# Re-timing the transfers and the layernorm of an attention and gate kernel on one core

## The chip, the core and the metric

The kernel runs on one core of a Trainium2 chip. The metric is the device time of one execution in microseconds (us). Times called a span run from the first to the last instruction of one profiled execution. Engines are named as in the profile: PE (matmul), PEld (its weight loads), DVE (vector), ACT (activation), POOL (GpSimd), SP (the sync engine, whose queue issues most DMAs).

## The reference

One input x of 2048 tokens by 512 is normalised, and the result feeds two branches whose product is added to x:

```python
xn = layernorm(x)                                  # over 512, no scale and no shift
q  = xn @ wq                                       # 512 -> 32 heads of 128
k, v = the last W = 512 rows of k_cache, v_cache   # 8 groups, each for 4 heads
p  = softmax(q k^T * 128 ** -0.5)                  # per head, 512 keys, no mask
s  = concat_heads(p v) @ wo                        # 4096 -> 512
g  = silu(silu(xn @ w1) @ w2)                      # 512 -> 1792 -> 512
out = x + s * g
```

Inputs and output are bfloat16.

## The kernel before

**Tiling.** The 2048 tokens are four blocks of 512 (`BLK`), each of four tiles of 128 (`BLKT`). For every block the normalised x lies transposed in `xnT[b]`, with features on partitions. Work is counted in 128 steps: step s handles block b = s // 32 and head h = s % 32.

**What a step does on PE.** `score(s, j)` multiplies query tile j with the keys into `sc_ps`; ACT takes the exp into `p_all[s]` and the row sums into `den[s]`. `normalise` divides `p_all` by the sums on DVE, two tiles at a time. `flip(s)` transposes `p_all[s]` into `pT[s]` by one DMA on the SP queue, issued in step s + 1. `pv_units(s)` multiplies pT with the values; it runs in step s + 3 (`LAG`). `q_units(s + 2)` computes the queries of the step after next. The `p_all`, `qT` and `pT` slots rotate over three buffers.

**Fill.** Between these, `pump(n)` takes matmuls from a list. In the 32 steps of the first block these are the gate branch (`mlp_units`) of blocks 1 to 3: 56 `h_unit` (xn @ w1, 14 chunks of four matmuls, each evacuated by a tanh on ACT and a multiply on DVE into `hT`) and 56 `o_unit` (into `g_sb`) for each block, 10 or 11 per step. In the later steps they are the output matmuls (`out_units`) of the block before, four per step: for each tile 32 heads of oT times wo, then DVE multiplies by the gate and adds x, and the result is stored. The x for that addition (`x_e`) is loaded again by POOL.

**Block 0 ahead of the steps.** Its layernorm runs on loaded tiles, PE transposes them (`turn`, `keep`), and its gate branch runs whole. Warm-up matmuls fill PE until the data are there. The first four chunks of `h` are computed in halves of 256 tokens, so that the first half can start before tiles 2 and 3 are transposed.

**Layernorm.** `stats` is a pair of statistics instructions on DVE; `rstd_of` takes Sqrt on ACT and a reciprocal on DVE; `center` is one DVE instruction per tile; `flip_x` transposes a tile into `xnT` by DMA on SP. Statistics of blocks 2 and 3 run during block 0's gate output; all four centerings and flips of block 2 stand at the end of step 0, those of block 3 at the end of step 1. The x blocks take their buffers from the `pT` slots.

**Loads and order.** `load_head_group(g)` loads keys (a transposing DMA), wq and values of a group on SP; groups 0 to 2 before the steps, the others at the end of the odd steps 1 to 9. `load_wo` loads wo in six parts on POOL's queue into the places that w1, w2 and hT leave. The order on PE, ACT, DVE and SP is written out by hand (`manual_schedule`), each engine executing in that order; POOL's was left to the planner.

Of the kernel before, what the change touches and what calls it, by code (L numbers as in the profile page):

```python
# [9 lines left out]
P = 128  # L10
# [6 lines left out]
LAG = 3  # L17
# [5 lines left out]
def kernel(  # L23
# [41 lines left out]
    make_identity(nc, ident)  # L65
    eps = const.tile([P, 1], FP32, name="eps")
    nc.vector.memset(eps, 1e-5)

    wq_sb = [res.tile([P, ND, REP * DH], BF16, name=f"wq{g}") for g in range(HKV)]
    kT = [res.tile([P, W], BF16, name=f"kT{g}") for g in range(HKV)]  # L70
    v_sb = [res.tile([P, NKC, DH], BF16, name=f"v{g}") for g in range(HKV)]
    xnT = [res.tile([P, ND, BLK], BF16, name=f"xnT{b}") for b in range(NBLK)]
    g_sb = [res.tile([P, BLKT, D], BF16, name=f"g{b}") for b in range(NBLK)]

# [9 lines left out]

    x_blk = {}

    def load_x(b):
        x_blk[b] = work.tile([P, BLKT, D], BF16, name="x_blk", tag="pT", bufs=3)  # L90
        if b == 0:
            for j in range(BLKT):
                nc.sync.dma_start(x_blk[b][:, j, :], x2[ds(j * P, P), :])
        else:
            nc.sync.dma_start(
                x_blk[b], x2[ds(b * BLK, BLK), :].rearrange("(j p) d -> p j d", p=P)
            )

    mv = res.tile([P, NBLK * BLKT, nc.vector.BN_AGGR_DIM], FP32, name="mv")
    rstd = res.tile([P, NBLK * BLKT], FP32, name="rstd")  # L100
# [1 line left out]
    def stats(b, j):  # L102
        st = work.tile([P, nc.vector.BN_STATS_DIM], FP32, name="st", bufs=4)
        nc.vector.bn_stats(out=st, in_=x_blk[b][:, j, :])  # L104
        nc.vector.bn_aggr(out=mv[:, b * BLKT + j, :], in_=st)  # L105

    def rstd_of(t0, n):
        nc.scalar.activation(
            rstd[:, t0 : t0 + n], mv[:, t0 : t0 + n, 1], ACT.Sqrt, bias=eps, scale=1.0
        )  # L110
        nc.vector.reciprocal(rstd[:, t0 : t0 + n], rstd[:, t0 : t0 + n])

    def center(b, j):
        t = b * BLKT + j
# [39 lines left out]
    def mlp_units(b, tag_of):  # L154

        cur = {}

        def h_unit(f, c):
            if (f, c) == (0, 0):
                new_hT(b)  # L160
            if c == 0:
                cur["ps"] = ps.tile([P, BLK], FP32, name="h_ps", tag=tag_of(f), bufs=PS_BUFS[tag_of(f)])
            h_mm(cur["ps"], b, f, c, 0, BLK)
            if c == ND - 1:
                h_evac(cur["ps"], b, f)

        def o_unit(j, f):
            if f == 0:
                cur["ps"] = ps.tile([P, D], FP32, name="oB_ps", tag=tag_of(j), bufs=PS_BUFS[tag_of(j)])
            nc.tensor.matmul(  # L170
                cur["ps"],
                hT[b][f // 2][:, f % 2, j * P : (j + 1) * P],
                w2_sb[f // FH][:, f % FH, :],
                start=(f == 0),
                stop=(f == NFC - 1),
            )
            if f == NFC - 1:

                th = work.tile([P, D], BF16, name="th", bufs=2)
                nc.scalar.activation(th, cur["ps"], ACT.Tanh, scale=0.25)  # L180
                nc.vector.scalar_tensor_tensor(
                    out=g_sb[b][:, j, :], in0=th, scalar=1.0, in1=cur["ps"], op0=ALU.add, op1=ALU.mult
                )

        hs = [lambda f=f, c=c: h_unit(f, c) for f in range(NFC) for c in range(ND)]
        os_ = [lambda j=j, f=f: o_unit(j, f) for j in range(BLKT) for f in range(NFC)]
        return hs, os_

# [80 lines left out]
                return t[:, h - lo, :]  # L269
        raise KeyError(h)  # L270

    def load_wo(lo, n, tag):
        t = reg.tile([P, n, D], BF16, name=f"wo{lo}", tag=tag)
        nc.gpsimd.dma_start(t, A_wo[ds(lo * DH, n * DH), :].rearrange("(h p) n -> p h n", p=P))
        wo_t.append((lo, n, t))

    def out_units(b):
        units = []
# [35 lines left out]
    wqv = A_wq.rearrange("(c p) n -> p c n", p=P)  # L314
    warm = const.tile([P, BLK], BF16, name="warm")
    nc.gpsimd.memset(warm, 0.0)

    with tc.manual_schedule(engines={ENG.PE, ENG.Activation, ENG.DVE, ENG.SP}):

        load_x(0)  # L320
        for i in range(2):
            nc.sync.dma_start(w1_sb[i], w1v[:, :, i * FH * P : (i + 1) * FH * P])
        load_x(1)
        for i in range(2):
            nc.sync.dma_start(w2_sb[i], w2v[:, i * FH : (i + 1) * FH, :])
        load_x(2)
        load_head_group(0)
        load_x(3)
        load_head_group(1)


        warm_ps = ps.tile([P, BLK], FP32, name="warm_ps", tag="o", bufs=1)
# [14 lines left out]

        stats(0, 0)
        stats(0, 1)
        rstd_of(0, 2)  # L350
        center(0, 0)
        center(0, 1)
        stats(0, 2)
        stats(0, 3)
        warm_up(11)
        t0 = turn(0)
        warm_up(2)
        t1 = turn(1)
        keep(nc.scalar, t0, 0)
        keep(nc.vector, t1, 1)  # L360
        warm_up(3)
        rstd_of(2, 2)
        center(0, 2)
        center(0, 3)


        new_hT(0)
        HB = BLK // 2
        NEARLY = 4
        early = [ps.tile([P, BLK], FP32, name="h_ps", tag="sc", bufs=PS_BUFS["sc"]) for _ in range(NEARLY)]  # L370
        for f in range(NEARLY):
            for c in range(ND):
                h_mm(early[f], 0, f, c, 0, HB)
            if f == 2:
                t2 = turn(2)
                t3 = turn(3)
                keep(nc.scalar, t2, 2)
                keep(nc.vector, t3, 3)
# [6 lines left out]
        for i, u in enumerate(hs[NEARLY * ND :]):  # L385
            u()
            f, c = divmod(i + NEARLY * ND, ND)
            if c == ND - 1 and f in (5, 7, 9, 11):
                stats(1, (f - 5) // 2)
        for i, u in enumerate(os_):  # L390
            u()
            if i == 2:
                rstd_of(BLKT, BLKT)
                for j in range(BLKT):
                    center(1, j)
                    flip_x(1, j)
            if i % 6 == 4 and i // 6 < 2 * BLKT:
                b, j = divmod(i // 6, BLKT)
                stats(2 + b, j)
            if i == 40:  # L400
                for q in q_units(0):
                    q()
            if i == 49:
                for q in q_units(1):
                    q()
        rstd_of(2 * BLKT, 2 * BLKT)
        load_head_group(2)


        fill = []  # L410
# [10 lines left out]
                    fill.pop(0)()  # L421
                    done += 1

        wo_plan = {HQ: [(14, 7, "big2")], HQ + 2: [(21, 7, "big3")], HQ + 3: [(28, 2, "pair0"), (30, 2, "pair1")]}
        wo_first = False
        for s in range(NSTEP):
            b, h = divmod(s, HQ)
# [27 lines left out]
            pump(cut[4])  # L455
            score(s, 3)
            pump(cut[5])
            if s in (0, 1):
                for j in range(BLKT):
                    center(2 + s, j)  # L460
                    flip_x(2 + s, j)
            if s % 2 == 1 and 3 + s // 2 < HKV:
                load_head_group(3 + s // 2)
            if not wo_first and b == 0 and done >= n_mlp - BLKT * NFC:
                load_wo(0, 7, "big0")
                load_wo(7, 7, "big1")
                wo_first = True
            for args in wo_plan.get(s, []):
                load_wo(*args)

# [1 line left out]
        s = NSTEP  # L472
        normalise(s - 1, 2, 3)
        flip(s - 1)
        for i in range(LAG):
            for u in pv_units(s - LAG + i):
                u()
            pump(8)
        pump(len(fill))


# [28 lines left out]
```

## Time and profile before

| what | value |
|---|---|
| median of 9 runs | 575.68 us (573.91 to 576.65) |
| profiled execution, its time | 574.93 us |
| its span | 573.2 us |
| PE busy | 549.7 us (96%) |
| DVE busy | 440.8 us (77%) |
| ACT busy | 386.3 us (67%) |
| POOL busy | 21.8 us (4%) |
| queue of SP and other hardware-generated DMAs | 81.29 MB, 74.8% of 16 engines |
| queue of POOL's DMAs | 7.87 MB, 5.2% |

Busy shares are means over the span. The busy tenths show the span in 40 slices of 14.3 us, where 9 means 90% or more. A row of the timeline has the start in us, the duration, the engine, the line, the operation, the tiles, a count, and in brackets the idle time before it and what ended that. SPq and POOL rows of DMAs are the issue, not the transfer; the transfer's end is given as time to landing. The granted clock (PEclk) is 1.00 at full speed.

### The profile page before, as it was taken

The page shows a single profiled execution, that of the slowest core. Times are in us where ns is not written, and L with a number is a line of the kernel's source. Part 1 is how long each engine was busy: PE and PEld are TensorE (multiplying, and loading weights), DVE is VectorE, ACT ScalarE, POOL GpSimd, SP SyncE. Part 2 cuts the span into 40 slices and gives each one's busy share as a digit, 9 for nine tenths or more (in the row PEclk, how much of TensorE's full clock was granted, in tenths as well). Part 3 has the DMA queues.
Part 4 walks back from the last instruction along what each step waited for, and adds up shares of the span by engine and source line. Part 5 has one row for each costly group of instructions (what it writes and reads, how often), then busy time and mean ns, then how long its engine had stood idle before and what let it go on. Part 6 is the DMA issues. An engine that isn't in the chain of part 4 may idle for free.

```text
span 573.2 us, 8179 instructions
## 1 busy us (share of the span) xinstructions
PE 549.7 (96%) x2527; PEld 252.2 (44%) x2576; DVE 440.8 (77%) x1185; ACT 386.3 (67%) x1108; POOL 21.8 (4%) x41
## 2 busy tenths in 40 slices
PE   8987699999999989999999999999999999999897
PEld 4433244444444434444444444444444444444345
DVE  5978467886787658888888878888888888888622
ACT  4657465775686657777777777777777777777400
POOL 0000000000000110000000000000000000000000
PEclk9999799999999989999999999999999999999999
DMA  8926999656578798989888888998988897989900
GB/s 285 248 73 111 192 179 215 119 100 119 108 164 165 134 258 160 166 151 168 157 171 160 169 148 171 156 173 155 173 148 165 151 178 148 180 148 171 166 27 29
DMA packets 293836, 89.68 MB, mean 156 GB/s; under 512 B 282272, under 2 KB 291872, under 8 KB 293792
## 3 DMA queue, kind: packets, MB, share of 16 engines
q1 hardware_dynamic: 291328, 81.29, 74.8%
q0 software_dynamic: 2464, 7.87, 5.2%
q8 instruction: 20, 0.33, 0.2%
q14 instruction: 24, 0.20, 0.1%
HBM read 17.30 MB, written 2.10 MB: 34 GB/s over the span
## 4 chain that ended last, share of the span: by engine, by line
PE 86%; DMA 5%; DVE 5%; ACT 2%; issue 1%; SPq 0%; ACTq 0%
PE sc_ps L222 19%; PE s_ps L286 18%; PE o_ps L254 18%; PE q_ps L203 18%; PE oB_ps L170 6%; PE h_ps L138 6%; DMA pT<-p_all 4%; DVE hT L150 2%; DVE st L104 1%; DMA w<-in_B_w_dram 1%; DVE x_blk L115 1%; ACT th L149 1%; ACT p_all L225 0%; DVE mv L105 0%; DVE p_all L237 0%
## 5 line engine op out<-in xcount | busy, mean ns | idle before, releaser
L225 ACT ACTIVATE p_all<-sc_ps 128x512 bf16<-128x512 f32 x512 | 305.0, 597 | 118.3 <-PE sc_ps L222 106.5
L222 PE MATMUL sc_ps<-kT,qT 128*128 128x512 bf16 x512 | 195.2, 382 | 0.7
L237 DVE TENSOR_SCALAR p_all<-p_all,rden 128x512 bf16<-128x512 bf16 x512 | 158.6, 352 | 9.1
L254 PE MATMUL o_ps<-pT,v 128*128 128x512 bf16 x498 | 135.3, 382 | 9.7 <-DMA pT<-p_all 9.3
L286 PE MATMUL s_ps<-wo,oT 128*128 128x512 bf16 (+1 forms) x533 | 141.3, 368 | 0.6
L203 PE MATMUL q_ps<-xnT,wq 128*128 128x512 bf16 x500 | 134.9, 379 | 0.6 <-DVE qT L212 0.2
L259 DVE CAST oT<-o_ps 128x512 bf16<-128x512 f32 x128 | 88.3, 690 | 50.6 <-PE o_ps L254 48.1
L225 ACT ACTIVATION_READ_ACCUMULATOR p_all<-sc_ps 128x1 f32 x512 | 100.7, 197 | 0.0
L212 DVE CAST qT<-q_ps 128x512 bf16<-128x512 f32 x128 | 87.9, 686 | 3.2 <-PE q_ps L203 3.2
L254 PEld LDWEIGHTS <-v 128*128 128x128 bf16 x512 | 49.9, 98 | 71.3 <-DMA pT<-p_all 6.7
L286 PEld LDWEIGHTS <-oT 128*128 128x128 bf16 x544 | 53.4, 98 | 58.2 <-issue 1.1
L222 PEld LDWEIGHTS <-qT 128*128 128x128 bf16 x512 | 50.4, 98 | 64.6 <-issue 5.3
L203 PEld LDWEIGHTS <-wq 128*128 128x128 bf16 x512 | 50.2, 98 | 61.9 <-issue 2.3
L138 PE MATMUL h_ps<-xnT,w 128*128 128x512 bf16 (+1 forms) x236 | 65.5, 370 | 6.5 <-DVE hT L150 5.5
L170 PE MATMUL oB_ps<-w,hT 128*128 128x512 bf16 x216 | 62.8, 379 | 0.3
L235 DVE RECIPROCAL rden<-den 128x2 f32<-128x2 f32 x256 | 40.6, 159 | 15.8 <-ACT p_all L225 15.8
L150 DVE SCALAR_TENSOR_TENSOR hT<-th,h_ps 128x512 bf16<-128x512 bf16 x56 | 37.6, 682 | 18.8 <-ACT th L149 18.2
L149 ACT ACTIVATE th<-h_ps 128x512 bf16<-128x512 f32 x56 | 33.4, 598 | 9.4 <-PE h_ps L138 7.1
L138 PEld LDWEIGHTS <-w 128*128 128x128 bf16 x240 | 23.6, 99 | 29.8 <-issue 4.8
L170 PEld LDWEIGHTS <-hT 128*128 128x128 bf16 x224 | 21.9, 98 | 26.5 <-DVE hT L150 0.3
L299 DVE TENSOR_TENSOR sg<-s_ps,g 128x512 f32<-128x512 f32 (+1 forms) x17 | 11.1, 655 | 18.4 <-PE s_ps L286 18.4
L180 ACT ACTIVATE th<-oB_ps 128x512 bf16<-128x512 f32 x16 | 9.5, 595 | 15.6 <-PE oB_ps L170 14.7
(28 smaller groups left out, 85.7 us busy)
## 6 DMA issues: line engine op xcount, KB each, us to landing
wq<-in_A_wq_dram SPq DMA_DIRECT2D x8, 512.0 KB, 4.4
w<-in_B_w_dram SPq DMA_DIRECT2D x4, 896.0 KB, 8.8
wo<-in_A_wo_dram POOLq DMA_DIRECT2D x4, 896.0 KB, 8.3
pT<-p_all SPq DMA_TRANSPOSE x128, 4.5
x_e<-in_A_x_dram POOLq DMA_DIRECT2D x16, 128.0 KB, 3.5
x_blk<-in_A_x_dram SPq DMA_DIRECT2D x3, 512.0 KB, 8.2
out_dram<-x_e POOLq DMA_DIRECT2D x12, 128.0 KB, 2.2
v<-in_A_v_cache_dram SPq DMA_DIRECT2D x8, 128.0 KB, 4.4
```

Source lines behind the costliest of these rows:

```text
L138: nc.tensor.matmul(h_ps[:, lo : lo + n], w1_sb[f // FH][:, c, (f % FH) * P : (f % FH + 1) * P], xnT[b][:, c, lo : lo + n], start=(c == 0), ...
L150: nc.vector.scalar_tensor_tensor(out=hT[b][f // 2][:, f % 2, :], in0=th, scalar=1.0, in1=h_ps, op0=ALU.add, op1=ALU.mult)
L170: nc.tensor.matmul(cur["ps"], hT[b][f // 2][:, f % 2, j * P : (j + 1) * P], w2_sb[f // FH][:, f % FH, :], start=(f == 0), stop=(f == NFC - 1),
L203: nc.tensor.matmul(cur["ps"], wq_sb[h // REP][:, c, (h % REP) * DH : (h % REP + 1) * DH], xnT[b][:, c, :], start=(c == 0), stop=(c == ND - 1),
L212: nc.vector.tensor_copy(qT[s], cur["ps"])
L222: nc.tensor.matmul(sc, qT[s][:, j * P : (j + 1) * P], kT[h // REP], start=True, stop=True)
L225: nc.scalar.activation(p_all[s][:, :, j, :], sc.rearrange("p (kc q) -> p kc q", q=P), ACT.Exp, scale=INV_SQRT_DH, accum_out=den[s][:, j : ...
L235: nc.vector.reciprocal(rden, den[s][:, j0 : j1 + 1])
L237: nc.vector.tensor_scalar_mul(p_all[s][:, :, j, :], p_all[s][:, :, j, :], rden[:, j - j0 : j - j0 + 1])
L254: nc.tensor.matmul(cur["ps"], v_sb[h // REP][:, kc, :], pT[s][:, kc, :], start=(kc == 0), stop=(kc == NKC - 1))
L259: nc.vector.tensor_copy(oT[s], cur["ps"])
L286: nc.tensor.matmul(cur["ps"], oT[b * HQ + h][:, j * P : (j + 1) * P], wo_of(h)[:, lo : lo + n], start=(h == 0), stop=(h == HQ - 1),)
```

## The change

The x blocks move from the pT slots to the slots that the gates take later (`g_sb[b]` is allocated under the same tag when its first gate is due). Block 0's x comes in four loads, two on SP's queue and two on ACT's; the first half of w1 is cut into six chunks on SP and the seventh on ACT's queue. Six early chunks of h instead of four are computed in halves, two of them in the PSUM places of q and o. A tanh of one column stands on ACT before the first real one. Block 0 keeps Sqrt and reciprocal (`rstd_early`); blocks 1 to 3 add epsilon and raise to -0.5 on POOL. Statistics, power, centering and flip of block 2 are spread over steps 0 to 8, those of block 3 over steps 9 to 17. Key groups 2 to 7 load at the end of steps 1, 5, 9, 13, 17 and 21, group 1 before the steps. wo comes in ten loads of two to four heads on SP's queue, after steps 27 to 30 and 32 to 36. POOL's order is written out as well. In the tail 6 and 14 output matmuls stand before the last two pv groups, where there were 8 and 8, and none after the last but the remaining list.

```diff
+    def new_x(b):
+        x_blk[b] = res.tile([P, BLKT, D], BF16, name=f"x{b}", tag=f"g{b}")
...
-        x_blk[b] = work.tile([P, BLKT, D], BF16, name="x_blk", tag="pT", bufs=3)
...
-    def rstd_of(t0, n):
+    def rstd_early(t0, n):
         nc.scalar.activation(
             rstd[:, t0 : t0 + n], mv[:, t0 : t0 + n, 1], ACT.Sqrt, bias=eps, scale=1.0
         )
         nc.vector.reciprocal(rstd[:, t0 : t0 + n], rstd[:, t0 : t0 + n])
+    def rstd_of(b):
+        r = rstd[:, b * BLKT : (b + 1) * BLKT]
+        nc.gpsimd.tensor_scalar(
+            out=r, in0=mv[:, b * BLKT : (b + 1) * BLKT, 1], scalar1=1e-5, scalar2=None, op0=ALU.add
+        )
+        nc.gpsimd.tensor_tensor(out=r, in0=r, in1=nhalf, op=ALU.pow)
...
-    def load_wo(lo, n, tag):
-        t = reg.tile([P, n, D], BF16, name=f"wo{lo}", tag=tag)
-        nc.gpsimd.dma_start(t, A_wo[ds(lo * DH, n * DH), :].rearrange("(h p) n -> p h n", p=P))
-        wo_t.append((lo, n, t))
+    def load_wo(h0, n):
+        for lo, m, t in wo_t:
+            if lo <= h0 < lo + m:
+                nc.sync.dma_start(
+                    t[:, h0 - lo : h0 - lo + n, :],
+                    A_wo[ds(h0 * DH, n * DH), :].rearrange("(h p) n -> p h n", p=P),
+                )
...
-        load_x(0)
-        for i in range(2):
-            nc.sync.dma_start(w1_sb[i], w1v[:, :, i * FH * P : (i + 1) * FH * P])
+        for j in range(BLKT):
+            (nc.scalar if j % 2 else nc.sync).dma_start(x_blk[0][:, j, :], x0v[:, j, :])
+        NE = NEARLY * P
+        nc.sync.dma_start(w1_sb[0][:, :, 0:NE], w1v[:, :, 0:NE])
+        nc.scalar.dma_start(w1_sb[0][:, :, NE:], w1v[:, :, NE : FH * P])
+        nc.sync.dma_start(w1_sb[1], w1v[:, :, FH * P :])
         load_x(1)
...
         load_x(2)
+        load_x(3)
         load_head_group(0)
-        load_x(3)
-        load_head_group(1)
...
         stats(0, 0)
         stats(0, 1)
-        rstd_of(0, 2)
+        stats(0, 2)
+        rstd_early(0, 2)
         center(0, 0)
         center(0, 1)
-        stats(0, 2)
         stats(0, 3)
...
-        rstd_of(2, 2)
+        rstd_early(2, 2)
+        nc.scalar.activation(scratch, eps, ACT.Tanh)
...
-        NEARLY = 4
-        early = [ps.tile([P, BLK], FP32, name="h_ps", tag="sc", bufs=PS_BUFS["sc"]) for _ in range(NEARLY)]
+        early = [
+            ps.tile([P, BLK], FP32, name="h_ps", tag=t, bufs=PS_BUFS[t]) for t in ("sc", "sc", "sc", "sc", "q", "o")
+        ]
...
             if i == 2:
-                rstd_of(BLKT, BLKT)
-                for j in range(BLKT):
-                    center(1, j)
-                    flip_x(1, j)
-            if i % 6 == 4 and i // 6 < 2 * BLKT:
-                b, j = divmod(i // 6, BLKT)
-                stats(2 + b, j)
+                rstd_of(1)
+            if i % 2 == 0 and 8 <= i < 8 + 2 * BLKT:
+                center(1, (i - 8) // 2)
+                flip_x(1, (i - 8) // 2)
...
-        rstd_of(2 * BLKT, 2 * BLKT)
-        load_head_group(2)
+        load_head_group(1)
...
+        wo_plan = {
+            HQ - 5: [(0, 4)],
+            HQ - 4: [(4, 3)],
+            HQ - 3: [(7, 4)],
+            HQ - 2: [(11, 3)],
+            HQ: [(14, 4)],
+            HQ + 1: [(18, 3)],
+            HQ + 2: [(21, 4)],
+            HQ + 3: [(25, 3)],
+            HQ + 4: [(28, 2), (30, 2)],
+        }
...
-            if s in (0, 1):
-                for j in range(BLKT):
-                    center(2 + s, j)
-                    flip_x(2 + s, j)
-            if s % 2 == 1 and 3 + s // 2 < HKV:
-                load_head_group(3 + s // 2)
+            for b2, s0 in ((2, 0), (3, 9)):
+                if s0 <= s < s0 + BLKT:
+                    stats(b2, s - s0)
+                if s == s0 + BLKT:
+                    rstd_of(b2)
+                if s0 + BLKT < s <= s0 + 2 * BLKT:
+                    center(b2, s - s0 - BLKT - 1)
+                    flip_x(b2, s - s0 - BLKT - 1)
+            if s % REP == 1 and s < HQ and s // REP + 2 < HKV:
+                load_head_group(s // REP + 2)
...
-        for i in range(LAG):
+        for i, n in enumerate((6, 14, 0)):
             for u in pv_units(s - LAG + i):
                 u()
-            pump(8)
+            pump(n)
         pump(len(fill))
```

## The prediction

> **What bounds the kernel now.** I read the page first: the busy tenths of PE, the granted clock, the DMA row and the shares of the chain that ended last.
>
> ```profile
> PE   8987699999999989999999999999999999999897
> ...
> PEclk9999799999999989999999999999999999999999
> DMA  8926999656578798989888888998988897989900
> ...
> PE 86%; DMA 5%; DVE 5%; ACT 2%; issue 1%; SPq 0%; ACTq 0%
> ```
>
> PE is the bound: from about 75 us on it stands at 9, with one weak slice near 207 us. What can be won lies in the weak slices: the first five (0 to 72 us), that one, and the last three. In an undisturbed step of the later blocks PE takes 3.45 us for 16 matmuls, 0.2155 us each; a step of the first block has 18 to 23 matmuls. A step starts where the timeline shows the first weight load from its qT. Cut at these starts, the windows give (first the early steps 0 to 5, then steps 11 to 13, then 32 to 34, with the 200 us of steady state last; columns: stretch, length, busy time of PE, PEld, DVE, ACT, POOL, clock, DMA share, GB/s):
>
> ```profile
> 35.59:41.69 6.10, 4.05 (x19) 1.76 (x18) 2.36 (x6) 5.62 (x11) 0.00 (x0) 1.00 0.01 2
> 41.69:47.03 5.34, 4.26 (x21) 1.85 (x19) 5.04 (x15) 4.14 (x14) 0.00 (x0) 1.00 0.25 51
> 47.03:52.82 5.79, 3.99 (x19) 1.76 (x19) 5.11 (x14) 4.01 (x13) 0.00 (x0) 1.00 0.85 127
> 52.82:57.78 4.96, 4.96 (x24) 2.24 (x23) 3.80 (x9) 3.75 (x11) 0.00 (x0) 1.00 0.57 119
> 57.78:69.58 11.80, 6.96 (x22) 2.64 (x22) 5.41 (x15) 4.31 (x13) 0.00 (x0) 0.75 0.89 201
> 69.58:75.01 5.43, 5.43 (x24) 2.39 (x23) 3.73 (x10) 3.52 (x11) 0.00 (x0) 0.91 1.17 197
> 99.18:104.15 4.97, 4.92 (x24) 2.26 (x24) 4.47 (x11) 4.13 (x13) 0.00 (x0) 1.00 0.85 154
> 108.90:113.86 4.96, 4.91 (x24) 2.25 (x23) 4.85 (x14) 3.72 (x13) 0.00 (x0) 1.00 0.50 92
> 205.39:213.05 7.66, 4.91 (x18) 1.78 (x17) 3.71 (x12) 2.82 (x10) 0.00 (x0) 0.83 1.06 263
> 300.00:500.00 200.00, 199.05 (x910) 90.69 (x927) 170.13 (x478) 154.81 (x464) 7.61 (x14) 1.00 0.87 162
> ```
>
> Steps 0 to 5 hold 18+19+18+23+22+23 = 123 matmuls, 26.5 us of work, and last 39.4 us: 12.9 us are lost, 7.1 of them in step 4. Steps 33 and 34 lose 7.66+3.86-6.90 = 4.6 us (the second lasts 3.86 us by the same view). Steps 6 to 31 lose under 0.8 us together. The cause of step 4's loss is in the timeline of the SP queue, with the PE row that ends the wait:
>
> ```profile
> 48.65 2.76 SPq L243 DMA_TRANSPOSE pT<-p_all  x1
> 51.50 5.16 SPq L125 DMA_TRANSPOSE xnT<-x_blk  x4
> 56.71 1.25 SPq L128 DMA_TRANSPOSE kT<-in_A_k_cache_dram  x1
> 58.02 0.57 SPq L131 DMA_DIRECT2D wq<-in_A_wq_dram  x1
> 58.63 0.51 SPq L132 DMA_DIRECT2D v<-in_A_v_cache_dram  x1
> 59.24 5.55 SPq L243 DMA_TRANSPOSE pT<-p_all  x2
> 64.94 1.01 PE L254 MATMUL o_ps<-pT,v 128*128 128x512 bf16 x2 [4.62 <-DMA pT<-p_all]
> ```
>
> The transpose of step 1 stands on SP behind four transposes of x (5.16 us) and three loads of a key group (2.33 us). It goes out at 59.24 and PE waits for it until 64.94.
>
> **The change part by part.**
>
> *x in the gates' slots, layernorm spread.* The four x flips of blocks 2 and 3 leave steps 0 and 1 and come singly in steps 5 to 8 and 14 to 17; the third key group leaves step 1 and group 2 takes that place. In step 2 the transpose of step 1 then finds only one group ahead, about 2.4 us of issue, and PE reads it about 2 us into step 4; two steps (near 9 us) cover 2.4 us plus the usual landing of 4.5 us. So the 7.1 us of step 4 go, and the 0.5 us of slow clock in step 5. Step 0 lost 2.2 us while ACT loaded two tables (1.28 us each, at 36.62 and 38.24) around the Sqrt of blocks 2 and 3, with the first exp held till 39.53; now POOL does that power, and exp and tanh ran in turn without a load before, so that goes too. Steps 1 and 2 lost 3.2 us to bursts of four centerings (1.38 us each) on DVE. In their place DVE gets one statistics pair per step in steps 0 to 3 (0.69+0.18 = 0.87 us): step 1 has 5.04-1.38+0.87 = 4.5 us of DVE for 4.09 us of PE, step 2 5.11-1.38+0.87 = 4.6 for 3.88. That leaves 1.2 us of lag; with the filling of the pipe in step 0 I take 2.0 us (from 0.8, if PSUM buffers absorb the lag, to 4.0, if DVE's gaps of 0.03 to 0.06 us between instructions count fully). Gain: 12.9-2.0 = 10.9 us.
>
> *The same for block 3, steps 9 to 17.* New work on DVE where there was none: step 11 then has 4.47+0.87 = 5.3 us for 4.96, step 12 4.09+0.87 for 4.74, and step 13 is full at 4.85. I put 0.8 us on it (0, if the lag is made up in the steps without statistics, to 2.5). The eight single flips cost SP 1.22 us each beside a pT of 2.0 us in a step of 4.9, and with a key group's 2.3 in steps 5 and 17 SP has 5.5 us for 4.9: late by 0.6 us against some 4 us of slack there, so nothing.
>
> *rstd on POOL.* Three pairs of 128x4 operations. POOL shows 0.28 us for an affine select and 0.10 to 0.53 us for memsets, and nothing of a power; I take 1 us a pair (0.3 to 5). DVE waits in order at the next centering: in block 0 six matmuls (1.3 us) after the pair, in steps 5 and 14 a whole step later. Behind it stand gates and q casts, which have some us of room in block 0 since eight statistics pairs (7 us) leave that place. So nothing is lost up to about 5 us. [...]
>
> *wo on SP, in pieces.* Before, POOL issued four wo loads at 197.44 to 202.62 (18 heads, 2.36 MB) and a transpose that lands in 4.5 us took 10.4:
>
> ```profile
> 197.44 0.75 POOL L274 DMA_DIRECT2D wo<-in_A_wo_dram  x1 [19.33 <-PE oB_ps L170]
> ...
> 202.62 0.93 POOL L274 DMA_DIRECT2D wo<-in_A_wo_dram  x1 [0.71 <-PE sc_ps L222]
> DMA to landing us min/median/max: 4.2/4.5/10.4
> ```
>
> After, these 2.36 MB go out behind the flips of steps 32 to 36, later than before. The DMA share of 0.87 leaves 0.45 us free in a step of 3.45. The POOL queue moved 7.87 MB in 5.2% of 573.2 us, 3.8 us per MB: 8.9 us; minus 5 x 0.45 makes a backlog of 6.7 us. By the timeline a pT is issued 1.6 us into the next step and read 1.3 us into the step two further on, 6.6 us later; with 4.5 us to land it has 2.2 us of slack. PE then waits 4.4 us in all. By the fastest stretch of plain loads, 339 GB/s from 8 to 22 us, it is 7.0-2.2-2.2 = 2.6. I take 3.5, both rows being equally near. [...] Gain 4.6-3.5 = 1.1 us. Pieces of steps 27 to 30 run beside 4.9 us steps with 4 to 5 us of slack: nothing.
>
> *The head.* Two x loads instead of four (0.42 us each) stand on SP before w1, whose landing at 7.93 released the first h matmul at 7.98. But xnT's second quarter came at 7.44+0.39 = 7.83 by DVE; statistics are reordered, which brings that to about 7.6. Gain 0.35. Six early groups instead of four cover the wait for the last quarter (0.36), and the tanh table (1.28 us at 10.32) moves ahead of need, which ends the gap of 0.64 us before 12.98. Sum 1.4 (0.5 to 2.2). ACT's three DMA issues, 1.3 us, come before a table that ended at 2.02 and is needed at 4.65: hidden. The w1 remainder is read near 13 us: hidden.
>
> *The tail.* The last pT lands when it lands; 20 output matmuls instead of 16 run before it, into a PE gap of 1.12 us: 4 x 0.2155 = 0.9 us.
>
> **Sum:** 1.4+10.9-0.8+1.1+0.9 = 13.5 us. The profiled execution took 574.93 us (span 573.2 and 1.7 around it): 561.4. It lies 0.75 us under the median of 575.68, which gives 562.2 us.
>
> **Rivals.**
> [...]
> (b) *DVE becomes the bound in the steps that got statistics.* Both upper ends: 2.0+1.7 more, 566. For it: 4.85 of 4.96 us in step 13. Against: steps 11 and 12 have spare.
> (c) *wo vanishes and DVE's lag is absorbed:* 3.5+1.2+0.8 less, 557.
> (d) *POOL's power is slow, and DVE stands at the centering.* Cover is 5 us in steps 5 and 14 and some 8 in block 0; a pair of L us costs 2(L-5)+(L-8). It eats 13.5 us at L = 10.5, and at 12 the kernel takes 580. Against: no POOL row is over 1.1 us.
> That x's own removal does nothing is hardly possible: the 5.16 us of flips are no longer ahead of that transpose.
>
> **How the numbers follow.** Main case 0.62 (own range 559.5 to 565), (a) 0.13, (b) 0.10, (c) 0.10, (d) or a like stall 0.05. The range 557.5 to 568 leaves out (d) and the ends of (a) and (c). A measurement here tells about 0.2%, 1.15 us, from nothing. Faster 0.94, same 0.02, slower 0.04.
>
> **What would show it.** Steps 0 to 5 within 29 us instead of 39, no PE wait over 2.5 us there; two ACT tables in all; POOL pairs under 5 us; PE waits for pT in steps 34 to 39 of 2.5 to 4.5 us in portions with the clock at 1.00; first h matmul at 7.6; no gap before the last o_ps. Wrong if DVE waits for POOL, or if pT lands over 8 us after issue in those steps.

## The result and the profile after

The changed kernel takes 567.35 us (median of 10 runs, 565.2 to 570.04) where the kernel before takes 574.89 us (31 runs shared by all comparisons, 571.54 to 576.65). The ratio is 0.9862, with a 95% interval of 0.9847 to 0.9878. The gain is 7.5 us of a predicted 13.5; the time lies inside the predicted range of 557.5 to 568, near its upper end, and outside the main case's own 559.5 to 565. The profiled execution took 565.44 us, with a span of 563.1 us, 10.1 us less than the span before.

The page of the kernel after, with the busy tenths of PE, the granted clock, the DMA row and the chain that ended last by engine:

```profile
PE   7998999999999997999999999999999999999997
...
PEclk8999999999999999999999999999999999999999
DMA  8739597878758899888888878888979797988800
...
PE 87%; DMA 6%; DVE 4%; ACT 1%; issue 1%; SPq 0%; ACTq 0%
```

The third to fifth slices (29 to 72 us), 8, 7 and 6 before and with a low clock in the fifth, are now 9, 8 and 9. One weak slice is left, the sixteenth, near 215 us: it is the stage in which wo is loaded. The first slice lost a tenth, in PE and in the clock.

The windows of the kernel after are cut where a step loads its first weights from qT: steps 0 to 5, then steps 11 and 13, then 37 to 39. Columns as before: stretch, length, busy time of PE, PEld, DVE, ACT and POOL, granted clock, DMA share, GB/s.

```profile
36.36:40.30 3.94, 3.89 (x19) 1.75 (x19) 2.30 (x5) 2.76 (x8) 0.00 (x0) 1.00 0.52 158
40.30:45.16 4.86, 4.26 (x21) 1.84 (x20) 4.50 (x13) 4.15 (x14) 0.00 (x0) 1.00 0.16 31
45.16:50.45 5.29, 4.04 (x20) 1.76 (x19) 4.57 (x12) 4.00 (x13) 0.00 (x0) 1.00 1.12 186
50.45:55.41 4.96, 4.91 (x23) 2.25 (x23) 4.38 (x11) 3.78 (x11) 0.00 (x0) 1.00 1.04 214
55.41:60.16 4.75, 4.75 (x24) 2.16 (x22) 4.64 (x14) 3.89 (x11) 1.43 (x2) 1.00 0.31 59
60.16:65.12 4.96, 4.91 (x23) 2.25 (x23) 4.85 (x15) 3.71 (x13) 0.00 (x0) 1.00 0.66 126
89.30:94.84 5.54, 5.12 (x24) 2.24 (x23) 5.38 (x15) 4.12 (x13) 0.00 (x0) 1.00 0.96 202
99.59:105.03 5.44, 5.13 (x25) 2.23 (x24) 5.30 (x15) 4.20 (x14) 1.42 (x2) 1.00 0.48 92
210.45:215.01 4.56, 3.63 (x18) 1.48 (x17) 2.83 (x9) 2.57 (x10) 0.00 (x0) 1.00 1.09 246
215.01:219.07 4.06, 3.58 (x17) 1.48 (x17) 2.83 (x9) 2.57 (x10) 0.00 (x0) 1.00 1.07 238
219.07:224.83 5.76, 3.63 (x18) 1.49 (x17) 2.83 (x9) 2.57 (x10) 0.00 (x0) 1.00 1.10 175
```

Steps 0 to 5 last 28.76 us (65.12 − 36.36) instead of 39.4; step 4 lasts 4.75 us instead of 11.80. Steps 11 and 13 now have 5.38 and 5.30 us of DVE and last longer than the 4.96 us they took before. Steps 37 to 39 last 14.38 us where three undisturbed ones take 10.35, with the clock at 1.00 and the DMA share above 1.

The same accounting over the whole span, each loss being a stretch's length less its matmuls at 0.2157 us:

| part | before | after | difference |
|---|---|---|---|
| start of step 0 | 35.59 | 36.36 | +0.8 |
| lost in steps 0 to 5 | 12.9 | 2.24 | −10.7 |
| lost in steps 11 to 17 | 0.36 | 1.48 | +1.1 |
| lost in steps 32 to 40 | 4.63 | 4.04 | −0.6 |
| start of step 127 to the end | 39.41 | 38.68 | −0.7 |

The sum is −10.1 us, the difference of the spans. The time gains less than the span for two reasons that can be counted: what lies around the span is 2.3 us after and 1.7 before, and the profiled execution is 1.9 us under the median of its runs. The second has to do with the clock. The granted clock is on record for each of the ten runs: the three at 0.996 to 1.000 took 565.2 to 565.44 us, the six at 0.993 and 0.994 took 566.55 to 567.72, and the one at 0.991 took 570.04. One stretch of 3.41 us at half clock, as the profiled execution has it, lowers this figure by 0.003.

Three more views of the kernel after. First the timeline of the SP queue at the place that cost most before, with the PE row that reads the transpose:

```profile
43.24 1.99 SPq L255 DMA_TRANSPOSE pT<-p_all  x1
45.27 1.69 SPq L138 DMA_TRANSPOSE kT<-in_A_k_cache_dram  x1
47.01 0.58 SPq L141 DMA_DIRECT2D wq<-in_A_wq_dram  x1
47.64 1.08 SPq L142 DMA_DIRECT2D v<-in_A_v_cache_dram  x1
48.81 3.09 SPq L255 DMA_TRANSPOSE pT<-p_all  x1
...
57.78 0.59 PE L266 MATMUL o_ps<-pT,v 128*128 128x512 bf16 x2
```

The transpose of step 1 stands behind one key group only and goes out at 48.81 instead of 59.24; PE reads it at 57.78 without a wait. The POOL timeline and the DVE row that waited for it:

```profile
26.41 0.23 POOL L118 TENSOR_SCALAR rstd<-mv 128x4 f32<-128x4 f32 x1 [24.69 <-DVE mv L107]
26.72 1.04 POOL L121 TENSOR_TENSOR rstd<-rstd,nhalf 128x4 f32<-128x4 f32 x1
27.80 1.06 DVE L125 TENSOR_SCALAR x<-x,mv,rstd 128x512 bf16<-128x512 bf16 x3 [1.48 <-POOL rstd L121]
```

The first power of the kernel takes 1.04 us, and so does the one in step 4. DVE waited 1.48 us for it, once. Last the PE timeline, its head and its two longest waits in the wo stage (the bracket has the idle time before the row and what ended it):

```profile
1.45 3.21 PE L361 MATMUL warm_ps<-warm 128*128 128x512 bf16 x8 [1.45 <-POOL warm L334]
6.59 0.72 PE L366 MATMUL t_ps<-ident,x 128*128 128x128 bf16 x8 [1.94 <-DVE x L125]
8.46 3.12 PE L148 MATMUL h_ps<-xnT,w 128*128 128x256 bf16 x16 [0.65 <-DMA w<-in_B_w_dram]
...
213.05 1.04 PE L266 MATMUL o_ps<-pT,v 128*128 128x512 bf16 x4 [0.93 <-DMA pT<-p_all]
...
222.87 1.04 PE L266 MATMUL o_ps<-pT,v 128*128 128x512 bf16 x4 [2.13 <-DMA pT<-p_all]
```

The head of the kernel before, for comparison:

```profile
1.46 4.60 PE L336 MATMUL warm_ps<-warm 128*128 128x512 bf16 x11 [1.46 <-POOL warm L316]
...
7.98 1.48 PE L138 MATMUL h_ps<-xnT,w 128*128 128x256 bf16 x12 [0.39 <-DMA w<-in_B_w_dram]
```

The change also cuts the warm-up matmuls, which the list of edits leaves out: 8 stand ahead of t_ps and 2 behind, where there were 11, 2 and 3. The eight end at 4.66, PE then stands for 1.94 us until x is centred, and the clock is at half from 7.54 for 3.41 us. The first matmul on h comes at 8.46 (7.98 before) and still waits for w1. In the wo stage a wait of 2.13 us left the clock at 1.00. The slowest transpose lands in 6.6 us, where it was 10.4.

### The profile page after: what moved, and what is told of

It reads as the page before. It is cut to its first block, busy times and chain, and to the rows that moved or that the text cites. A ratio compares the mean times of both kernels' runs of the same rounds, so it can differ in the third digit from the quotient of the medians.

```text
span 563.1 us, 8185 instructions
## 1 busy us (share of the span) xinstructions
PE 545.2 (97%) x2529; PEld 251.6 (45%) x2578; DVE 439.1 (78%) x1184; ACT 380.3 (68%) x1103; POOL 20.7 (4%) x41
## 4 chain that ended last, share of the span: by engine, by line
PE 87%; DMA 6%; DVE 4%; ACT 1%; issue 1%; SPq 0%; ACTq 0%
PE sc_ps L234 19%; PE o_ps L266 18%; PE s_ps L304 18%; PE q_ps L215 18%; PE oB_ps L182 8%; PE h_ps L148 6%; DMA pT<-p_all 4%; DVE hT L160 2%; DMA w<-in_B_w_dram 1%; ACT th L159 1%; DVE st L106 1%; DVE p_all L249 1%; ACT p_all L237 0%; DVE mv L107 0%; DVE qT L224 0%
## 5 line engine op out<-in xcount | busy, mean ns | idle before, releaser
L304 PE MATMUL s_ps<-wo,oT 128*128 128x512 bf16 (+1 forms) x531 | 139.9, 366 | 0.6
L317 DVE TENSOR_TENSOR sg<-s_ps,gate 128x512 f32<-128x512 f32 (+1 forms) x17 | 11.1, 655 | 17.6 <-PE s_ps L304 17.6
```

Source lines behind the costliest of these rows:

```text
L304: nc.tensor.matmul(cur["ps"], oT[b * HQ + h][:, j * P : (j + 1) * P], wo_of(h)[:, lo : lo + n], start=(h == 0), stop=(h == HQ - 1),)
```

## The experiments

Four theories were put to the test: that the gain of steps 0 to 5 is the order on SP (the rival: the pT buffers that x no longer takes); that the spread statistics are what DVE loses in steps 0 to 17; that the loss in the wo stage is a backlog of bytes from which a slack is taken off (rivals: the queue, the buffers' place); and that the head loses its gain by the idle time of PE and the clock (rival: the division of w1 and the order of loads). Below, e1 is the first kernel, the change with four more warm-ups. Most later kernels start from it, to keep the head's clock out of the comparison; these are marked "on e1".

### The head: warm-ups

```diff
-        warm_up(8)
+        warm_up(12)
```

> The changed kernel with 12 warm-up matmuls instead of 8 ahead of the first transposes, nothing else. Theory A: the changed kernel loses at the head because PE rests 1.94 us (4.65 to 6.59) and the granted clock then falls to half for 3.4 us. The clock then stays at 1.00 up to 12 us, step 0 starts at about 34.5 us instead of 36.36, and the time is 2 us under the changed kernel's 567.35. Rival: the head is late because x lands later on two queues; then step 0 starts within 0.4 us of 36.36 and the time is the same.

Measured: 563.92 us (4 runs, 563.68 to 564.02), ratio 0.9805 (0.979 to 0.9819), against 0.9862 after: 0.57% of 575, about 3.3 us better than the change itself, and the best median of the kernels that compute the reference. Its PE timeline:

```profile
1.45 4.67 PE L361 MATMUL warm_ps<-warm 128*128 128x512 bf16 x12 [1.45 <-POOL warm L334]
6.52 0.72 PE L366 MATMUL t_ps<-ident,x 128*128 128x128 bf16 x8 [0.39 <-DVE x L125]
9.36 1.92 PE L148 MATMUL h_ps<-xnT,w 128*128 128x256 bf16 x16 [1.70 <-DMA w<-in_B_w_dram]
```

The gap before t_ps is 0.39 us instead of 1.94, and the clock stays at 1.00. Though w1 comes later here than after (9.36 against 8.46), step 0 begins at 36.06, 0.3 us earlier. The rest of the span's 1.4 us is the wo stage, which lost 2.80 us here and which the edit does not touch. So step 0 stands where the rival had it, not at the 34.5 us of the theory; the time fell as the theory had it. Half the clock does cost time: from the first h matmul to step 0 it takes 26.70 us here and 27.90 in the change, 1.2 us more; the later w1 hides most of that here. The four runs of e1 were granted 0.999 to 1.000 and lie within 0.34 us of each other; those of the change were granted 0.991 to 1.000 and lie within 4.8 us. So the 3.4 us between the medians go with the clock. That it fell in the head in those runs too is inferred from the edit, since they have no trace.

The warm-ups don't always hold the clock. Six later kernels have the same head as e1 in the first 14 us; of their 18 runs 10 were granted 0.996 or 0.997, as one stretch at half clock would give, and none less. In the profiles of three of them it fell at the wait for w1.

### The head: all of it undone

```diff
-            (nc.scalar if j % 2 else nc.sync).dma_start(x_blk[0][:, j, :], x0v[:, j, :])
-        NE = NEARLY * P
-        nc.sync.dma_start(w1_sb[0][:, :, 0:NE], w1v[:, :, 0:NE])
-        nc.scalar.dma_start(w1_sb[0][:, :, NE:], w1v[:, :, NE : FH * P])
+            nc.sync.dma_start(x_blk[0][:, j, :], x0v[:, j, :])
+        nc.sync.dma_start(w1_sb[0], w1v[:, :, 0 : FH * P])
...
-        warm_up(8)
+        warm_up(11)
```

The other lines of the edit put back NEARLY = 4, the order of the statistics, the later warm-ups (2 and 3) and leave out the early tanh.

> The changed kernel with the whole head of the kernel before: four x loads and an undivided w1 on SP, four early chunks, its order of statistics, its 11, 2 and 3 warm-ups, no early tanh. Theory A: the new head costs 0.8 us in the profile and more in other runs; step 0 starts at 35.6 us and the time falls by 0.8 to 2 us under 567.35. Rival: the new head gains 1.4 us as the prediction had it, and the profiled execution was an outlier; then the time rises by about 1.4 us.

Measured: 565.58 us (565.05 to 566.72), ratio 0.9837 (0.9819 to 0.9854); step 0 at 35.81. The old head is not slower than the new one: its interval overlaps that of the change and its median is lower by 1.8 us. The predicted gain of 1.4 us in the head was not there. From the first h matmul to step 0 it takes 27.24 us here and 26.70 in e1, which differs in the head alone: the six early chunks and the early tanh bring 0.5 us in these two profiles.

### The head: w1's first half undivided (on e1)

```diff
-        nc.sync.dma_start(w1_sb[0][:, :, 0:NE], w1v[:, :, 0:NE])
-        nc.scalar.dma_start(w1_sb[0][:, :, NE:], w1v[:, :, NE : FH * P])
+        nc.sync.dma_start(w1_sb[0], w1v[:, :, 0 : FH * P])
```

> e1_warm with the first half of w1 in one load on SP, as before the change; x stays on two queues. If the seventh chunk on ACT's queue (rows of 256 bytes) is what delays the first six, the first h matmul starts at 8.0 to 8.4 us instead of 9.36 and the time falls by about 1 us. If the landing of w1 is set by all the loads that are queued together, the start stays within 8.4 to 9.6 us and the time within 0.5 us of 563.9.

Measured: 564.97 us, ratio 0.9817 (0.9787 to 0.9847), the same as e1 within the intervals. The PE row of this kernel, then that of the kernel with the old head:

```profile
8.69 1.92 PE L148 MATMUL h_ps<-xnT,w 128*128 128x256 bf16 x16 [1.00 <-DMA w<-in_B_w_dram]
```

```profile
8.57 1.48 PE L148 MATMUL h_ps<-xnT,w 128*128 128x256 bf16 x12 [1.16 <-DMA w<-in_B_w_dram]
```

In the eleven profiles with the loads as the change has them, the first h matmul starts between 8.46 and 10.07 us; with the undivided half at 8.69, with the old head at 8.57, before at 7.98. The piece of w1 in the new order is smaller and is issued earlier (1.65 instead of 2.60 us), yet lands no earlier. One profile inside the range of the others doesn't show the chunk on ACT's queue to be the cause. The three profiles with an undivided half lie at 7.98 to 8.69 us, though, and ten of the eleven with the divided one at 8.89 or later, which points to the division. From 4 to 8 us the DMA share is 1.01 after and 0.95 before, so an earlier issue found the DMA engines busy. Neither was tested by itself in more than one profile, and the cause stays open.

### Steps 0 to 5: the bunches put back

x keeps its own slots, so that the pT buffers are free as in the change; only the order goes back: four centerings and flips stand at the end of steps 0 and 1, and both powers ahead of the steps. Key groups stay at every fourth step.

```diff
-            for b2, s0 in ((2, 0), (3, 9)):
-                if s0 <= s < s0 + BLKT:
-                    stats(b2, s - s0)
-                if s == s0 + BLKT:
-                    rstd_of(b2)
-                if s0 + BLKT < s <= s0 + 2 * BLKT:
-                    center(b2, s - s0 - BLKT - 1)
-                    flip_x(b2, s - s0 - BLKT - 1)
+            if s in (0, 1):
+                for j in range(BLKT):
+                    center(2 + s, j)
+                    flip_x(2 + s, j)
```

Statistics go back into block 0's gate output.

> The changed kernel with the spreading alone undone: statistics of blocks 2 and 3 in block 0's gate output, both powers on POOL before the steps, and the four centerings and flips of each block together at the end of steps 0 and 1, as in the kernel before. x stays in the gates' slots and the key groups at every fourth step. Theory D: the stall of step 4 comes from the order on SP. The transpose of step 1 again stands behind four flips (5.2 us) and a key group (2.4 us), so step 4 loses 4 us or more and the clock falls near 60 us. Rival: it came from the pT slots that the x blocks took; with x elsewhere steps 3 to 5 lose under 1 us.

Measured: 577.37 us (one run; the kernel before beside it 573.13 to 576.95), so the whole gain is gone. Its SP timeline, and the PE row that waited:

```profile
52.12 2.07 SPq L255 DMA_TRANSPOSE pT<-p_all  x1
54.28 5.45 SPq L135 DMA_TRANSPOSE xnT<-x  x4
59.79 1.25 SPq L138 DMA_TRANSPOSE kT<-in_A_k_cache_dram  x1
61.09 0.57 SPq L141 DMA_DIRECT2D wq<-in_A_wq_dram  x1
61.71 0.51 SPq L142 DMA_DIRECT2D v<-in_A_v_cache_dram  x1
62.31 3.55 SPq L255 DMA_TRANSPOSE pT<-p_all  x1
```

```profile
68.02 1.01 PE L266 MATMUL o_ps<-pT,v 128*128 128x512 bf16 x2 [5.07 <-DMA pT<-p_all]
```

This is the picture of before: the transpose goes out at 62.31 behind 5.45 us of flips and 2.3 us of loads, PE waits 5.07 us, and the clock falls to half for 6.83 us at 65.59. Steps 0 to 5 lose 11.2 us with the pT buffers free. So it is the order on SP, not the buffers. The profile is one execution, whose head too fell to half clock, for 6.83 us at 7.57.

### The statistics put back into block 0

```diff
+            if 18 <= i < 50 and (i - 18) % 4 == 0:
+                stats(2 + (i - 18) // 16, (i - 18) // 4 % 4)
...
-                if s0 <= s < s0 + BLKT:
-                    stats(b2, s - s0)
```

> The changed kernel with the eight statistics pairs of blocks 2 and 3 back in block 0's gate output, centerings and flips left where the change put them. Theory C: the statistics on DVE make the losses of steps 1 and 2 (2.2 us) and most of steps 11 to 15 (1.5 us); they fall to under 0.5 and 0.5 us and the time falls by 2.5 us. Rival: the losses come from the chain score, exp, hT that fills in the first steps; they stay above 1.5 us in steps 0 to 3, and the time falls by 1 us at most.

> e1_warm and e4_stats together: 12 warm-ups, and the statistics of blocks 2 and 3 in block 0's gate output. If the two gains add (e4_stats lost 1.9 us less in steps 0 to 17 than the changed kernel), the time is 562.0 us, 1.9 under e1_warm's 563.9, and the clock stays at 1.00. If the statistics only move the wait, it is within 0.5 us of 563.9.

Measured, the first on the change and the second on e1: 566.66 us (563.1 to 568.01), ratio 0.9843 (0.9804 to 0.9882), and 564.4 us, ratio 0.9814 (0.9784 to 0.9844). In both, steps 0 to 5 lose 1.38 us instead of 2.24 and steps 11 to 17 lose 0.44 instead of 1.5: the spread statistics cost 1.9 us there. But neither kernel is measurably faster than the one it starts from. In the second, step 0 starts 28.1 us after the first h matmul, in e1 26.7: the seven us of statistics delay block 0 by 1.4 us. Spread or not, they cost nearly the same (in these profiles). The profile of the first has in its head a wait of 2.44 us for w1 and, by windows, a slow clock:

```profile
9.50:13.00 3.50, 3.02 (x15) 2.16 (x16) 0.00 (x0) 0.00 (x0) 0.00 (x0) 0.50 1.08 367
```

Its step 0 starts at 40.50 for that.

### Sqrt instead of the power on POOL (on e1)

```diff
-        nc.gpsimd.tensor_scalar(
-            out=r, in0=mv[:, b * BLKT : (b + 1) * BLKT, 1], scalar1=1e-5, scalar2=None, op0=ALU.add
-        )
-        nc.gpsimd.tensor_tensor(out=r, in0=r, in1=nhalf, op=ALU.pow)
+        rstd_early(b * BLKT, BLKT)
```

> e1_warm with Sqrt on ACT and the reciprocal on DVE for blocks 1 to 3 instead of the power on POOL; the rest stays. Two table loads of 1.28 us per block come back, in steps 4 and 13 and in block 0. By the prediction's account (step 0 lost 2.2 us to them) steps 4 and 13 lose 1 to 2 us each and the time rises by 2 to 4 us over 563.9. Rival: ACT has the room (3.9 us of 4.75 in step 4) and the time rises by less than 1 us.

Measured: 567.85 us, ratio 0.9873 (0.9839 to 0.9907), 3.9 us above e1. The ACT timeline in step 13:

```profile
105.59 1.28 ACT L110 ACT_TABLE_LOAD   x1
106.88 0.30 ACT L110 ACTIVATE rstd<-mv,eps 128x4 f32<-128x4 f32 x1
107.19 1.28 ACT L234 ACT_TABLE_LOAD   x1
108.49 0.60 ACT L234 ACTIVATE p_all<-sc_ps 128x512 bf16<-128x512 f32 x1
```

ACT is away for 2.9 us (105.59 to 108.49). Of block 2's pair of tables nothing is lost in steps 4 and 5 and 0.6 us in step 8; of block 3's, step 14 loses 2.5 us. The power on POOL avoids both.

### wo: another queue, another place (on e1 and on the change)

```diff
-                nc.sync.dma_start(
+                nc.gpsimd.dma_start(
...
+            if s in wo_plan:
+                nc.gpsimd.tensor_copy(pace, den[s][:, 3:4])
```

> e1_warm with the ten wo pieces issued by POOL instead of SP, at the same steps (a POOL copy of one column of den of that step stands before each and holds it back). Theory B (amount of DMA work): the waits of steps 35 to 40 stay at 2.8 to 4.0 us and the time within 1 us of e1_warm's 563.9. Rival (order on the SP queue: each transpose is issued and served behind its piece): they fall below 1.5 us and the time falls by 2 us.

Measured: 567.07 us (563.93 to 570.06), ratio 0.9852 (0.9805 to 0.9899). In its profile (the 563.93 us run) steps 32 to 40 lose 3.33 us, inside what SP's queue gives; the transposes land in 6.9 to 8.6 us though no piece of wo is issued ahead of them on SP, and PE's longest wait for pT is 1.93 us. So in this profile the queue makes no difference. The other three runs are 3 to 6 us slower than the profiled one. They were granted 0.997 of the clock where it was granted 0.999, as one stretch at half clock would give; such a stretch cost 1.2 to 1.7 us in the profiled heads, and what else they lost isn't known.

```diff
-            HQ: [(14, 4)],
-            HQ + 1: [(18, 3)],
-            HQ + 2: [(21, 4)],
-            HQ + 3: [(25, 3)],
-            HQ + 4: [(28, 2), (30, 2)],
+            HQ - 1: [(14, 4)],
+            HQ: [(18, 4)],
+            HQ + 1: [(22, 3)],
+            HQ + 2: [(25, 4)],
+            HQ + 3: [(29, 3)],
...
+            if s == HQ - 1:
+                wo_t.append((14, 4, res.tile([P, 4, D], BF16, name="wo14", tag="xnT0")))
```

> The changed kernel, but wo heads 14 to 17 go into the place of xnT of block 0 after step 31, so that 14 heads instead of 18 are loaded from step 32 on (4, 3, 4, 3). Theory B: the waits of steps 37 to 39 (4.0 us in the changed kernel) are a backlog of DMA work; 0.52 MB less is about 2 us less, so steps 32 to 40 lose 1.5 to 2.5 us and the time falls by 2 us. Rival: each transpose behind a wo piece is late whatever the amount; the loss stays near 4 us, only a step earlier.

Measured: 566.14 us, ratio 0.9842 (0.9821 to 0.9864); steps 32 to 40 lose 3.68 us. That is no fall of the expected size. Kernels with the plan of the change lose between 2.45 and 4.04 us there, so a fall of less than that spread can't be seen. The transpose of step 31 had 0.75 to 0.8 us to spare in the change and in e1, here 0.04: the piece sent one step earlier used up slack before the stage began, which would explain the miss, but this is an inference from one profile.

### wo: the late bytes left out (on e1)

Two kernels load none or 9 of the 18 late heads and put other heads of wo in their place, so that what they compute is not the reference; the matmuls are as many.

```diff
+        h = h % 14
...
-            HQ: [(14, 4)],
-            HQ + 1: [(18, 3)],
-            HQ + 2: [(21, 4)],
-            HQ + 3: [(25, 3)],
-            HQ + 4: [(28, 2), (30, 2)],
```

```diff
+        h = h - 7 if 21 <= h < 28 else h - 2 if h >= 30 else h
...
-            HQ: [(14, 4)],
-            HQ + 1: [(18, 3)],
-            HQ + 2: [(21, 4)],
-            HQ + 3: [(25, 3)],
-            HQ + 4: [(28, 2), (30, 2)],
+            HQ: [(14, 2)],
+            HQ + 1: [(16, 2)],
+            HQ + 2: [(18, 2)],
+            HQ + 3: [(20, 1)],
+            HQ + 4: [(28, 2)],
```

> e1_warm without the loads of wo heads 14 to 31; their matmuls run on heads 0 to 13 again, so the output is another but PE's work is the same. Theory B: the waits of steps 32 to 40 are wholly the work of these 2.36 MB; they lose under 0.3 us instead of 2.8 to 4.0. Rival: the transposes' slack runs out by itself where steps shorten from 4.9 to 3.45 us; then 1 us or more stays.

> e1_warm with 9 of the 18 late wo heads loaded (2, 2, 2, 1, 2 after steps 32 to 36), the others' matmuls on loaded heads, so the output is another and PE's work the same. By the prediction's sum the backlog is 1.18 MB x 3.8 - 5 x 0.45 = 2.2 us, just the slack: loss under 0.5 us. If each piece costs by itself, whatever its size, the loss is near 3 us again.

Measured: spans 561.65 and 560.9 us (times 563.99 and 563.2, one run each). Steps 32 to 40 lose 0.02 us in both. Steps 36 and 37 with half the bytes, by windows:

```profile
208.68:212.13 3.45, 3.45 (x18) 1.57 (x16) 2.82 (x9) 2.67 (x10) 0.00 (x0) 1.00 1.12 206
212.13:215.58 3.45, 3.45 (x17) 1.57 (x16) 2.82 (x9) 2.71 (x10) 0.00 (x0) 1.00 1.12 217
```

and steps 37 and 38 of e1, with all of them:

```profile
210.17:214.44 4.27, 3.63 (x18) 1.49 (x16) 2.83 (x9) 2.57 (x10) 0.00 (x0) 1.00 1.11 241
214.44:219.86 5.42, 3.63 (x17) 1.48 (x16) 2.83 (x9) 2.56 (x10) 0.00 (x0) 1.00 1.13 235
```

The DMA share is as high with half the bytes, but PE takes 3.45 us a step: the transpose of step 36 lands 0.04 us before it is needed. Half the bytes leave 0.04 us of the slack and 0.02 us of loss; the second half costs all of the 2.80 us that e1 loses here. A loss proportional to the bytes would have given about 1.4 us at half. The times are not under e1's because both heads fell to half the clock, after waits of 2.41 and 2.08 us for w1.

### The tail as before (on e1)

```diff
-        for i, n in enumerate((6, 14, 0)):
+        for i, n in enumerate((8, 8, 8)):
```

> e1_warm with the tail's 8, 8 and 8 output matmuls of the kernel before instead of 6, 14 and 0. By the prediction the time rises by 0.9 us to 564.8. Rival: the last transposes move as well and the gap only shifts; then it stays within 0.4 us of 563.9.

Measured: 567.18 us, ratio 0.9864 (0.9832 to 0.9895). The time isn't comparable, because the clock of this kernel fell in the head for 3.41 us (after a wait of 1.93 us). The tail can be read by itself. The PE row of the kernel before, of this kernel and of the change:

```profile
544.23 1.04 PE L254 MATMUL o_ps<-pT,v 128*128 128x512 bf16 x4 [1.12 <-DMA pT<-p_all]
```

```profile
535.43 1.04 PE L266 MATMUL o_ps<-pT,v 128*128 128x512 bf16 x4 [1.87 <-DMA pT<-p_all]
```

```profile
535.23 1.04 PE L266 MATMUL o_ps<-pT,v 128*128 128x512 bf16 x4 [0.42 <-DMA pT<-p_all]
```

The three waits for pT in the tail sum to 2.5 us here and to 1.6 in e1: 0.9 us, the price of four matmuls. From the start of step 127 to the end it is 39.74 and 38.80 us. But the twelve profiles with the new tail lie between 38.37 and 39.94 us there (39.75 in the kernel of e1 with the statistics put back, whose tail is that of e1), so a difference of this size isn't shown by one pair. The last wait alone was 1.12 us before and 1.87 here, and 0 to 1.1 in those with the new tail.

## Why the prediction was right in sign and too large by 5 to 6 us

That the time lies inside the range is in part luck. 567.35 us is outside the main case and nearest to what rival (b) gave (566), but (b) didn't happen: DVE's steps lost near what the main case had. Nor did a much costlier wo stage, which (a) stands for among the chances: it lost 4.04 us where 3.5 were taken. What took the gain was the head, to which the prediction gave a gain of at least 0.5 us.

**Steps 0 to 5: right.** Predicted 10.9 us, measured 10.7, with 2.0 us left to lose and 2.24 lost. Of the 2.24 us, 0.86 goes when the statistics leave these steps and 1.38 stays; the prediction had 1.2 and 0.8. The mechanism was the transpose of step 1 behind four flips and a key group on SP; the bunches put back bring both the row and the wait back.

**Steps 9 to 17: right in cause, a little under.** Predicted 0.8 us more, measured 1.1. The kernels with the statistics put back lose only 0.44 us there, so it is their work on DVE.

**The power on POOL: right.** A pair taken at 1 us takes 1.27 to 1.43 us. The range also has room for a slow first call on POOL, which no run shows: the first power took 1.04 us like the later ones, and started 0.08 us after the addition had ended. DVE did wait for POOL, 1.48 us in block 0, which the prediction had named as a sign of being wrong; but from the first h matmul to step 0 it is 26.70 us with Sqrt in its place and 26.70 in e1, so this wait cost nothing. The Sqrt would cost 3.9 us in the time now, 3.0 of it in steps 8 and 14 of its profile.

**The wo stage: mechanism right, size off by 0.5 us.** Predicted loss 3.5 us, measured 4.04 in the change and 2.45 to 4.04 among kernels with the same plan; the gain is 0.6 us and not 1.1. That backlog less slack is the form of the sum is shown by half the bytes costing 0.02 us. The slack at the start was smaller than the 2.2 us taken: the transpose of step 31 had 0.78 us to spare (0.79 in the kernel without the late bytes, where that of step 32 had 2.05 again). The waits came in portions, the longest of 2.13 us, and the clock stayed at 1.00 as expected.

**The tail: 0.7 us for 0.9 in this pair of profiles,** within the spread of the tail from profile to profile, and so not shown.

**The head: this step failed.** The gain of 1.4 us was a loss of 0.8 us in the profile. Three things were wrong in it. First, the step took two fewer issues ahead of w1 on SP (2 × 0.42 us) for an earlier landing of w1; the issue came 0.95 us earlier and the landing came no earlier in any profile. The working counted the loads' place in the queue alone, though the DMA share was 0.95 from 4 to 8 us already. Second, it took 7.6 us for the first h matmul from xnT's second quarter alone, as though w1 would not be the last to come. Third, it costed the edit of the warm-ups at nothing by leaving it out: the change has 8 ahead of t_ps, 3.21 us of work that ends at 4.66, while x was centred at 6.5. After the gap of 1.94 us the clock is at half for 3.41 us. Four more warm-ups (4 × 0.4 us) close the gap. By single profiles the loss of 0.8 us is made up as follows: w1 later 0.5, half clock 1.2, early chunks and tanh −0.5 (1.0 was predicted for them), and −0.4 that is left over; the statistics of blocks 2 and 3, which left this stretch, would explain it. Over the runs the clock costs more: 0.993 to 0.994 was granted in the middle runs, 0.997 in the profiled one.

**The clock.** In the kernel before, a wait of 2.05 us left the clock at 1.00 and one of 2.75 us was followed by half clock, from 210.46 us on:

```profile
41.48 0.59 PE L138 MATMUL h_ps<-xnT,w 128*128 128x512 bf16 x2 [2.05 <-DVE hT L150]
...
209.82 1.30 PE L254 MATMUL o_ps<-pT,v 128*128 128x512 bf16 x4 [2.75 <-DMA pT<-p_all]
```

Length alone doesn't decide: in the other profiles waits of 1.93 to 2.44 us in the head brought the clock to half, one of 2.13 us in the wo stage did not. What fits the 14 profiles is idle time on a grid. In each of them the granted clock changes only at points that are whole multiples of 3.413 us apart (before: 17 of them at full clock from 5.66 to 63.68 us, then 2 at half, 41 at full, 1 at half). Add up PE's idle time between neighbouring points while the clock is full: in the nine stretches that ended in a fall before the end of the work it is 1.92 to 3.36 us, in all others 1.94 us or less, the four largest being 1.94, 1.88, 1.87 and 1.84. The 1.94 us of the change lie within one stretch, 4.13 to 7.54 us. The wait of 2.13 us is cut at 222.58 into 1.84 and 0.29, that of 2.05 us before 41.48 at 39.79 into 0.36 and 1.69. With the statistics put back on the change, waits of 1.38 and 2.44 us share a stretch that ends at 8.24 us with 2.09 us idle, and there it fell. The grid lies elsewhere in each profile (a point at 5.66 us before, at 4.13 in the change, at 8.24 with the statistics put back on it). By this reading a wait of about 2 us lowers the clock in one execution and not in another, as 1.93 us did in the kernel with the tail as before, and 1.93 us in the kernel with wo on POOL's queue did not. This is read from the records afterwards; no kernel was run to test it.

In sum, on the span: 2.2 us missed in the head, 0.25 in steps 0 to 5, 0.3 in 9 to 17, 0.5 in the wo stage and 0.2 in the tail are the 3.4 us between 13.5 and 10.1. The further 2.5 us between 10.1 and the 7.5 of the medians are the time around the span (0.6) and the profiled execution's place among its runs (1.9), which goes with the granted clock; the prediction took both to be as before. e1 shows that the change can have most of this when the clock stays full: it gains 10.9 us on the medians of its comparison (574.79 − 563.92). Later kernels with its head did not always keep the clock.

## What to carry to other kernels

On a queue that carries a transfer each step waits for, count the issue time of everything that stands ahead of that one transfer; here pacing the rest one per step brought 10.7 us, and moving wo to another queue nothing that shows. When a stage has slack, find the point up to which bytes are free before spreading them: here half of the late wo bytes lost 0.02 us and all of them 2.45 to 4.04. When a load at the start is moved, fill the wait anew: after waits of 1.93 to 2.41 us at the head of PE the clock was at half for 3.41 us, which cost 1.2 us between the first h matmul and step 0 in the change and 1.6 to 1.7 in three kernels where it fell later.

## What the runs showed of the hardware that was not expected

- A smaller first piece of w1, issued 0.95 us earlier, does not land earlier: the first h matmul at 8.46 to 10.07 us in eleven profiles, 7.98 and 8.57 with the old loads, 8.69 with the half undivided on the new order. The cause is open.
- In these profiles the granted clock changes on a grid of 3.413 us whose place differs from profile to profile (a point at 5.66 us before, at 4.13 in the change). It fell where PE stood idle 1.92 to 3.36 us between two grid points, in one wait or in two, and stayed full up to 1.88 us and once at 1.94. At half clock a second such stretch followed where PE stood idle 1.25 us or more in the first (four cases); in the change, with 0.65 us, none followed.
- One profile (a piece of wo in another place) has no clock row before 13.04 us; the 16 first h matmuls take 3.59 us there, 3.60 with the statistics put back on the change, where the clock is on record at 0.50, and 1.92 in e1. By that the clock was at half.
- The power on 128x4 elements takes POOL 1.04 us, the addition before it 0.23 to 0.39.
- Half of the late wo bytes leave PE at 3.45 us a step with the DMA share at 1.12; all of them, at 1.11 to 1.13, make steps of 4.27 and 5.42 us. Here the busy share of the DMA engines doesn't tell whether the stage is late.
